# Summing the next unit's first block ahead of this unit's last gelu, in a gated MLP built from seven-product block multiplications

## The chip, the cores and the metric

The kernel runs on one core of a Trainium2 chip. The metric is the time of one execution on the device in microseconds (us). Before the change the median was 542.64 us in three runs (541.96 to 542.75).

The engines: TensorE (PE; its weight loads stand separately as PEld), VectorE (DVE), ScalarE (ACT), GpSimd (POOL), and SyncE (SP), which issues the transfers. TensorE writes its products into PSUM, which the program uses as eight banks of 128 x 512 f32; the operands of its matmuls lie in SBUF. A "slot" is one of 52 buffers of a shared pool in SBUF, used again and again. fp32r is a 4-byte float type for matmuls.

## The reference

```python
# B, S, Dm, Df = 1, 2048, 1024, 3584; all bf16
def reference(x, w_gate, w_up, w_down):
    g = jnp.einsum("bsd,df->bsf", x, w_gate)
    u = jnp.einsum("bsd,df->bsf", x, w_up)
    h = _gelu(g) * u                      # tanh form
    return jnp.einsum("bsf,fd->bsd", h, w_down)
```

## The kernel before

The rows of x are taken in two passes (`ip` 0 and 1) of 1024. Each pass first makes h, in 14 units of 256 columns of the gate and up weights, and then multiplies by the down weights. A unit is a 2 x 2 block multiplication done with seven products instead of eight: sums and differences of blocks of x (`t1` to `t4`, and the cast `tb`) are multiplied with sums and differences of weight blocks (`s1` to `s4`, and the cast `sa`). GpSimd makes the weight sums of the next unit while this one runs. Two of the seven products take raw bf16 blocks, the others take fp32r. Everything exists for gate and for up, so a "product" below is two groups of four matmuls. `p1`, `u2` and `p5` are copies of products that ScalarE takes out of PSUM (`snap`).

The down projection is done in the same way, and for it 14 slices of the down weights have to be subtracted from each other once. Most of that is hidden in the first pass: in 12 of its units, ScalarE copies three raw halves of a slice into PSUM banks that are idle just then (`keep`), and VectorE subtracts from there into `m`. The second pass does none of this.

```python
def add(ps, other):
    g = new(dve, ps[0], other[0], ADD, "sum", dtype=f32)   # gate: VectorE, into a slot
    dve(ps[1], ps[1], other[1], ADD)                        # up: VectorE, in place in PSUM
    return g, ps[1]

# ... inside unit(...): e, c, d are pairs of PSUM banks
    e, c, d = banks
    aside(-2)
    g, up = add(c, p1)                    # the unit's first block: c holds raw products
    aside(-1)
    for i in GU:
        product(e[i], s["s2"][i], t["t2"], False)
    aside(0)
    keep(0, c[0])                         # ScalarE copies raw weights into c[0], VectorE subtracts
    # ... (first unit: another order)
    g = gelu(g)                           # ScalarE
    c11 = g, up
    times(2 * u, 0, *c11)                 # VectorE multiplies into h
    u2 = [snap(e[i], "u2") for i in GU]   # ScalarE copies PSUM to SBUF
    keep(1, c[0])
    keep(2, c[1])
    c = d
    for i in GU:
        product(c[i], s["s1"][i], t["t1"], True)
    p5 = [snap(c[i], "p5") for i in GU]   # ScalarE
    after_p5()
    for i in GU:
        product(e[i], s["s3"][i], t["t3"], False)
    # ... add e and p5 (VectorE)
    for i in GU:
        product(c[i], s["s4"][i], t["tb"], False)   # the "tb products": same banks as p5's source
    times(2 * u + 1, 1, gelu(g), up)
    aside(1)
    g, up = add(c, u2)
    ahead_of_p4()                         # raw products of the NEXT unit, and its p1 copies
    for i in GU:
        product(e[i], s["sa"][i], t["t4"], False)
    times(2 * u, 1, gelu(g), up)
    aside(2)
    times(2 * u + 1, 0, gelu(e[0]), e[1]) # the unit's last gelu and multiply

def keep_part(j, part, ps):
    ra, rb = wraw[j]
    # ... (part 0 takes a new tile made[j])
    a = (ra[:, N:], rb[:, N:], rb[:, :N])[part]
    b = (ra[:, :N], made[j][:, 0], made[j][:, 1])[part]
    nc.scalar.copy(out=ps, in_=a)
    dve(made[j][:, part], ps, b, SUB)
```

VectorE and TensorE keep the order in which the program is written. ScalarE's order is set by a scheduler, in most units; it comes out as gelu, raw copy, gelu, two u2 copies, two raw copies, two p5 copies, two `sa` casts.

## Time and profile before

| | before |
|---|---|
| time, median | 542.64 us |
| PE busy, share of the span | 535.1 us, 99% |
| DVE / ACT / POOL busy | 62% / 47% / 44% |
| first-pass unit, mean of 11 | 12.62 us |
| second-pass unit, mean of 12 | 12.56 us |

From the page of the kernel before: busy time, share of the span and instructions of each engine (its part 1), and the chain of work that ended last (its part 4).

```profile
PE 535.1 (99%) x2414; PEld 379.5 (70%) x2414; DVE 334.9 (62%) x524; ACT 255.4 (47%) x463; POOL 239.2 (44%) x215
...
PE 99%; ACT 0%; DVE 0%; issue 0%
PE bank L111 98%; PE bank L502 1%; PE bank L449 0%; ACT st L413 0%; DVE warm L433 0%
```

The chain is all matmuls. But busy time cannot tell whether matmuls follow each other as fast as they could. The Trainium skill, "Perfetto Trace Analysis", section "Identifying the Most-Contended Engine", says that matmul busy share is not a good measure of how close a kernel is to its roofline, since pipelined matmuls look smaller in the trace. PE busy is 12.56 us of a 12.56 us window in a unit of either pass, although a first-pass unit takes longer. So the single records of the trace were taken, and the distance from one matmul's start to the next was worked out. It is 216 ns for bf16 and 227 ns for fp32r nearly everywhere, but not in the last product of a unit (`t4` with `sa`), which ripples between 224 and 236 ns in both passes and is taken up at the end. The tb products differ between the passes: 10 of the 12 units with down weights are like the first row. (This is not a view of the profile: the numbers are differences of start times, and times between a copy's end and a start.)

```
kernel before                    end of the two p5 copies,    the first tb load   distances of the eight starts
                                 before the first tb matmul   leads its matmul by from one to the next (ns), sum
first pass, typical unit         209 ns and -277 ns           96 ns               251 237 233 236 224 231 236 233   1881
second pass, typical unit        1766 ns and 1026 ns          224 ns              226 227 227 226 227 227 226 230   1816
```

From the waits view of the kernel before. The columns are who waited for what: us in total, times, longest.

```profile
DVE hT L90 <- PE bank L111: 43.7, 25, 1.8
...
ACT bank L274 <- DVE sum L90: 20.5, 12, 1.7
...
PEld bank L111 <- issue: 2.0, 12, 0.2
```

The last line is the leak as this view shows it: twelve times, the weight load of an fp32r product began late, and the view has no engine to name for it ("issue"). The middle line is where the lateness starts: a ScalarE copy of raw weights into a bank waits 12 times 1.7 us for VectorE's sum.

From the timeline of the kernel before, one first-pass unit. The columns are start, duration, engine, line, operation, tiles out<-in, shapes, count, and in brackets the idle time just before with what ended it.

```profile
124.57 0.60 ACT L179 ACTIVATE g<-bank 128x512 f32<-128x512 f32 x1 [1.49 <-PE bank L111]
...
125.56 0.69 DVE L90 TENSOR_TENSOR hT<-g,bank 128x512 bf16<-128x512 f32 x1 [1.75 <-PE bank L111]
126.17 0.68 DVE L90 TENSOR_TENSOR sum<-bank,p 128x512 f32<-128x512 f32 x1
126.77 0.69 DVE L90 TENSOR_TENSOR bank<-bank,p 128x512 f32<-128x512 f32 x1
126.89 0.59 ACT L274 CAST bank<-raw 128x512 f32<-128x512 bf16 x1 [1.71 <-DVE sum L90]
...
127.94 1.06 ACT L107 COPY u<-bank 128x512 f32<-128x512 f32 x2
...
128.89 1.12 ACT L274 CAST bank<-raw 128x512 f32<-128x512 bf16 x2
...
129.93 1.08 ACT L107 COPY p<-bank 128x512 f32<-128x512 f32 x2
130.64 1.70 PEld L111 LDWEIGHTS bank<-tb,s 128*128 128x128 f32 x8 [0.17 <-issue]
130.73 2.04 PE L111 MATMUL bank<-tb,s 128*128 128x512 f32 x8
```

Read it from the bottom. The tb products overwrite a bank pair that the p5 copies must have read; the second copy, which frees the second bank, starts at 130.4 us and the first at 129.93, just before the load at 130.64. The p5 copies stand behind two raw copies, those behind the u2 copies, and all of it behind the first raw copy at 126.89, which stood idle for 1.71 us until VectorE had done the sum at 126.17. The sum in turn is queued behind the multiply `hT` at 125.56, for which VectorE had itself been idle for 1.75 us.

### The profile page before, as it was taken

What the parts mean: (1) busy time and instruction counts of PE and PEld (TensorE: products, weight loads), DVE (VectorE), ACT (ScalarE), POOL (GpSimd) and SP (SyncE); (2) the same over time, 40 slices, a digit from 0 to 9 for tenths busy, and PEclk for the clock granted to TensorE, in tenths of its full rate; (3) what the DMA queues carried; (4) which work ended last, traced back from release to release, by engine and by line L of the source; (5) the groups of instructions that cost most, each with busy time, mean ns of one, the idle gap of its engine ahead of it and who ended that gap; (6) DMA issues with size and microseconds to landing.
All of it is one profiled execution on the core that took longest, in us unless ns stands there. A gap on an engine that the chain in (4) does not pass through costs nothing.

```text
span 539.8 us, 7428 instructions
## 1 busy us (share of the span) xinstructions
PE 535.1 (99%) x2414; PEld 379.5 (70%) x2414; DVE 334.9 (62%) x524; ACT 255.4 (47%) x463; POOL 239.2 (44%) x215
## 2 busy tenths in 40 slices
PE   9999999999999999999999999999999999999997
PEld 5577777666677646888877667777777775488885
DVE  2986666666666895694945545445554459676730
ACT  3556666666656410255354555454555541114431
POOL 1079966677773500000097777777766600000000
PEclk9999999999999999999999999999999999999999
DMA  9766666666664899979772232233330059573751
GB/s 247 157 181 177 175 176 191 201 185 186 200 188 141 294 379 316 301 181 292 240 195 79 78 80 78 79 88 99 101 101 4 1 167 372 182 240 92 236 183 49
DMA packets 108133, 93.28 MB, mean 173 GB/s; under 512 B 17216, under 2 KB 92992, under 8 KB 108096
## 3 DMA queue, kind: packets, MB, share of 16 engines
q1 hardware_dynamic: 108096, 92.82, 58.8%
q8 instruction: 19, 0.31, 0.2%
q14 instruction: 18, 0.15, 0.1%
HBM read 74.45 MB, written 15.20 MB: 166 GB/s over the span
## 4 chain that ended last, share of the span: by engine, by line
PE 99%; ACT 0%; DVE 0%; issue 0%
PE bank L111 98%; PE bank L502 1%; PE bank L449 0%; ACT st L413 0%; DVE warm L433 0%
## 5 line engine op out<-in xcount | busy, mean ns | idle before, releaser
L93 POOL TENSOR_TENSOR s<-w 128x512 fp32r<-128x512 bf16 x102 | 120.0, 1198 | 165.1 <-DVE t L90 86.7
L111 PE MATMUL bank<-t,s 128*128 128x512 f32 x648 | 151.7, 390 | 0.0
L111 PEld LDWEIGHTS bank<-t,s 128*128 128x128 f32 x648 | 121.6, 188 | 25.5
L90 DVE TENSOR_TENSOR hT<-g,bank 128x512 bf16<-128x512 f32 x112 | 76.7, 687 | 92.9 <-ACT g L179 46.0
L111 PE MATMUL bank<-xT,w 128*128 128x512 bf16 (+1 forms) x504 | 111.9, 376 | 0.0
L107 ACT COPY p<-bank 128x512 f32<-128x512 f32 x124 | 70.6, 593 | 77.4 <-PE bank L111 77.1
L111 PEld LDWEIGHTS <-w 128*128 128x128 bf16 x504 | 47.0, 98 | 58.5 <-issue 6.9
L179 ACT ACTIVATE g<-sum 128x512 f32<-128x512 f32 x81 | 51.4, 635 | 29.8 <-DVE sum L90 28.6
L111 PE MATMUL bank<-q 128*128 128x512 f32 x240 | 58.9, 389 | 0.0
L111 PE MATMUL bank<-t,sa 128*128 128x512 f32 x216 | 58.8, 414 | 0.0
L93 POOL TENSOR_TENSOR s<-w,s 128x512 fp32r<-128x512 bf16 x50 | 57.8, 1181 | 0.0
L93 POOL TENSOR_TENSOR s<-s,w 128x512 fp32r<-128x512 f32 x50 | 57.0, 1162 | 0.0
L90 DVE TENSOR_TENSOR sum<-bank,p 128x512 f32<-128x512 f32 x54 | 37.0, 685 | 30.5 <-PE bank L111 30.5
L111 PE MATMUL bank<-tb,s 128*128 128x512 f32 x216 | 54.0, 392 | 0.0
L111 PEld LDWEIGHTS bank<-q 128*128 128x128 f32 x240 | 45.0, 188 | 9.4
L111 PE MATMUL bank<-raw,hT 128*128 128x512 bf16 x224 | 48.7, 379 | 0.0
L111 PEld LDWEIGHTS bank<-t,sa 128*128 128x128 f32 x216 | 40.7, 188 | 10.7
L111 PEld LDWEIGHTS bank<-tb,s 128*128 128x128 f32 x216 | 39.6, 188 | 9.9 <-issue 2.0
L102 ACT CAST tb<-raw 128x512 fp32r<-128x512 bf16 x28 | 17.2, 626 | 60.0 <-DMA raw<-in_w_down_dram 26.5
L90 DVE TENSOR_TENSOR q<-hT 128x512 fp32r<-128x512 bf16 x56 | 38.4, 686 | 4.5 <-PE bank L111 4.5
L111 PEld LDWEIGHTS <-hT 128*128 128x128 bf16 x224 | 21.8, 98 | 26.5 <-issue 0.5
L90 DVE TENSOR_TENSOR bank<-bank,p 128x512 f32<-128x512 f32 x54 | 37.4, 693 | 3.1 <-PE bank L111 3.1
(45 smaller groups left out, 454.7 us busy)
## 6 DMA issues: line engine op xcount, KB each, us to landing
raw<-in_w_down_dram SPq DMA_DIRECT2D x80, 256.0 KB, 4.8
q<-td SPq DMA_DIRECT2D x60, 256.0 KB, 5.0
w<-in_w_gate_dram SPq DMA_DIRECT2D x27, 512.0 KB, 5.9
w<-in_w_up_dram SPq DMA_DIRECT2D x27, 512.0 KB, 7.0
td<-m SPq DMA_DIRECT2D x12, 768.0 KB, 4.5
w<-td SPq DMA_DIRECT2D x6, 1024.0 KB, 9.7
out_dram<-st SPq DMA_DIRECT2D x32, 128.0 KB, 1.7
td<-w SPq DMA_DIRECT2D x2, 768.0 KB, 6.6
```

What stands on the lines that cost most here:

```text
L90: nc.vector.tensor_tensor(out=out, in0=a, in1=b, op=op)
L93: nc.gpsimd.tensor_tensor(out=out, in0=a, in1=b, op=op)
L102: nc.scalar.copy(out=t, in_=src)
L107: nc.scalar.copy(out=t, in_=ps)
L111: nc.tensor.matmul(ps, lhsT=lhs, rhs=rhs, start=start, stop=stop, skip_group_check=True)
L179: nc.scalar.activation(g, src, ACT.Gelu_apprx_tanh)
L502: nc.tensor.matmul(bank[3][:, :cols], lhsT=warm[:, :P], rhs=warm[:, :cols], start=True, stop=True)
```

## The change

The intent: the sum of the next unit's first block needs only the raw products and their p1 copies, and these are complete before the last product of this unit. It is put ahead of the last gelu and its multiply, into VectorE's idle time; then ScalarE's raw copy, whose bank the sum frees, moves up as well.

```diff
-    def unit(u, banks, xT, w, s, t, p1, after_p5, aside, keep, ahead_of_p4, snap_first):
+    def add(ps, other):                       # moved out of unit, otherwise the same
+        ...
+    def unit(u, banks, xT, w, s, t, c11, after_p5, aside, keep, ahead_of_p4, behind_p4, snap_first):
         ...
-        g, up = add(c, p1)
+        g, up = c11()
         ...
         times(2 * u, 1, gelu(g), up)
-        aside(2)
+        behind_p4()
         times(2 * u + 1, 0, gelu(e[0]), e[1])
 ...
+            def behind_p4():
+                if "p1" in nxt:
+                    nxt["c11"] = add(cc, nxt["p1"])
+
+            def c11():
+                return nxt.pop("c11", None) or add(cc, p1)
```

(`aside(2)` did nothing.) No operation is added or removed; the matmuls keep their order.

More of the change, by code (lines that the diff above doesn't have):

```diff
@@ L196, in raw_products @@
         return p1
-    def unit(u, banks, xT, w, s, t, p1, after_p5, aside, keep, ahead_of_p4, snap_first):
+    def add(ps, other):
+        g = new(dve, ps[0], other[0], ADD, "sum", dtype=f32)
+        dve(ps[1], ps[1], other[1], ADD)
+        return g, ps[1]
+    def unit(u, banks, xT, w, s, t, c11, after_p5, aside, keep, ahead_of_p4, behind_p4, snap_first):
         GU = range(2)
-        def add(ps, other):
-            g = new(dve, ps[0], other[0], ADD, "sum", dtype=f32)
-            dve(ps[1], ps[1], other[1], ADD)
-            return g, ps[1]
         e, c, d = banks
         aside(-2)
-        g, up = add(c, p1)
+        g, up = c11()
         aside(-1)
@@ L576 @@
             with tc.manual_schedule(engines={ENG.Activation}) if first else nullcontext():
-                unit(u, (e, cc, dd), xT, w, s, t, p1, prepare, aside, keep, ahead_of_p4, first)
+                unit(
+                    u, (e, cc, dd), xT, w, s, t, c11, prepare, aside, keep,
+                    ahead_of_p4, behind_p4, first,
+                )
             if u + 1 < NU:
```

## The prediction

> **What bounds the kernel.** TensorE. The page gives PE busy 535.1 us of a span of 539.8 (99%), full granted clock in every slice, and a chain of waits that is 98% matmuls of one helper line. The Trainium skill, "Perfetto Trace Analysis", section "Identifying the Most-Contended Engine", says that matmul busy share is a poor measure, since matmuls are pipelined; so I read the distance from one matmul's start to the next in the timeline: 216 ns for bf16, 227 for fp32r products, nearly everywhere, with one of about 418 at each change from bf16 to fp32r. The waits view has no matmul waiting for a semaphore. VectorE (62%) and ScalarE (47%) are spare.
>
> **The one leak.** The tb products (operands tb and s) differ between the passes. In the second, their eight distances add up to 1816 ns per unit. In the first, in 10 of 12 units, to about 1880: the first is 251 ns instead of 227, the next ones 231 to 238. Two more units have about 1838. The waits view shows the weight loads before them idle for "issue", 2.0 us in 12 times: they start only 96 ns ahead of the matmul, against 224 in the second pass. (The skill's "TensorE: Matmul & The Clock Gate", "Step-by-step: what each phase is for", says weight loads are pulled ahead of matmuls in flight; this trace agrees.) Reason: these products write banks that ScalarE's p5 copies must first have read. In the second pass those copies end 1766 and 1026 ns before the first tb matmul; in the first, 209 ns before and 277 ns after it. There ScalarE also makes three copies of raw down weights per unit (598 ns each), the first of which waits 1.71 us for VectorE's sum, queued behind the multiply after the unit's last gelu. Loss, worked out: 10 x 64 + 2 x 22 = 0.7 us, 0.13%.
>
> **What the change does.** No operation is added or removed. Sum (685 ns) and add in place (690 ns) move ahead of the last multiply (687 ns), into a stretch where VectorE idles 1.75 us; their operands are complete 2 us before the old place. The sum should end before the last gelu starts. The first raw copy then follows that gelu at once, the gelu of the sum runs 1.7 us earlier, the second copy can start sooner, and the p5 copies should end about 1.1 and 0.6 us before the first tb matmul, restoring the weight load's lead.
>
> Slot reuse shifts: some sums now wait for a Pool sum as well, some Pool sums for a DMA. I traced the targets: all about a unit back, long done. Matmul order is unchanged.
>
> **On the critical path:** only the 0.7 us, all in the first pass.
>
> **Predicted time:** 542.0 us, 8-in-10 range 541.2 to 542.8. Faster by over 2%: 0.005; within 2%: 0.985; slower by over 2%: 0.01.
>
> **Signs.** Right: ScalarE's wait for the sum before the raw copy (20.5 us, 12 times) almost gone; first-pass tb products at 1817 ns; the 2.0 us of "issue" idle gone; first-pass unit period from 12.63 to 12.56 us. Wrong: tb distances stay at 251 although the p5 copies end earlier (then contention is the cause), or new distances over 240 ns elsewhere.
>
> **What would make it wrong.** The 0.7 us is near the run-to-run spread (541.96 to 542.75), so times may hide it. A misjudged slot wait could stall Pool sums, which have about 2 us of room ahead of the tb products, and so TensorE.

## The result, and the profile after

Ratios are the mean time of one kernel's fast runs over the mean of the other's in the same rounds, so they are not quite the ratio of the medians quoted.

In the first comparison the changed kernel took 541.13 us (median of 4, 540.65 to 541.99) against 542.67 us before (4 runs), ratio 0.9976, 95% interval 0.9959 to 0.9994: within 2%, and a little faster. The profiles, from single executions:

| | before | after |
|---|---|---|
| first-pass unit, mean of 11 | 12.62 us | 12.56 us |
| second-pass unit, mean of 12 | 12.56 us | 12.56 us |
| tb products, typical first-pass unit: first distance | 251 ns | 227 ns |
| p5 copies end before the first tb matmul | 209 and -277 ns | 1313 and 826 ns |
| span of the profiled run | 539.8 us | 539.9 us |

From the page of the kernel after, its part 1:

```profile
PE 533.1 (99%) x2380; PEld 381.4 (71%) x2414; DVE 334.6 (62%) x524; ACT 260.0 (48%) x463; POOL 239.2 (44%) x215
```

PE busy is not down by 2 us because anything became cheaper: this trace holds 2380 of the 2414 matmuls, and all 2414 weight loads. 34 matmul records are missing, most of them the first matmul of the raw products of the next unit. A second trace of the same kernel (the first experiment) has all 2414, and PE busy 535.3 us.

From the waits view of the kernel after:

```profile
DVE hT L90 <- PE bank L111: 13.6, 24, 0.6
...
ACT g L179 <- DVE sum L90: 7.4, 6, 1.7
PEld L111 <- issue: 7.3, 28, 0.3
```

The line of ScalarE's raw copy waiting for the sum (20.5 us) is gone, and so is the "issue" idle of the fp32r loads (2.0 us). The last line above is another group, the loads of raw bf16 weights; it stood at 7.4 us before. VectorE's multiply waits 13.6 us instead of 43.7 for TensorE, since the sum now fills that time.

From the timeline of the kernel after, one first-pass unit:

```profile
136.75 0.68 DVE L90 TENSOR_TENSOR sum<-bank,p 128x512 f32<-128x512 f32 x1
...
137.65 0.60 ACT L179 ACTIVATE g<-bank 128x512 f32<-128x512 f32 x1 [1.54 <-PE bank L111]
...
138.14 0.59 ACT L272 CAST bank<-raw 128x512 f32<-128x512 bf16 x1
...
138.57 0.69 DVE L90 TENSOR_TENSOR hT<-g,bank 128x512 bf16<-128x512 f32 x1 [0.54 <-PE bank L111]
...
140.80 1.11 ACT L272 CAST bank<-raw 128x512 f32<-128x512 bf16 x2
...
141.84 1.08 ACT L107 COPY p<-bank 128x512 f32<-128x512 f32 x2
...
143.52 1.55 PEld L111 LDWEIGHTS bank<-tb,s 128*128 128x128 f32 x7
143.74 1.52 PE L111 MATMUL bank<-tb,s 128*128 128x512 f32 x6
```

The raw copy follows the last gelu at once, the p5 copies are done by 142.9, and the first load begins 0.22 us before its matmul, with no idle time before it.

Why then are the two profiled spans the same? The stages, from the starts of matmuls in the two traces:

```
stage, us                                              before    after    difference
start of the span to the first product with x           7.00      7.89     +0.89
first product with x to the first tb product            22.85     22.82    -0.03
first to 13th tb product (units of the first pass)      151.43    150.72   -0.71
13th to 14th (last unit, down projection, new pass)     100.31    100.24   -0.07
14th to 27th tb product (units of the second pass)      163.28    163.28    0.00
27th tb product to the end of the span                  94.92     94.92     0.00
```

One line of the timeline of each kernel shows the first stage, before and then after:

```profile
7.00 3.31 PE L111 MATMUL bank<-xT,w 128*128 128x256 bf16 x22
```

```profile
7.88 2.41 PE L111 MATMUL bank<-xT,w 128*128 128x256 bf16 x17
```

The start-up, which the change does not touch, took 0.89 us longer in the one execution that was profiled. Over the seven traces here without an added copy it lies between 6.96 and 7.96 us whatever the kernel. Behind it the changed kernel gains 0.81 us, 0.78 of it between the first tb product of the first pass and that of the second.

### The profile page after: what moved, and what is told of

Same layout as the page of the kernel before. It is cut to its first block, busy times and chain, and to the rows that moved or that the text cites. A ratio compares the mean times of both kernels' runs of the same rounds, so it can differ in the third digit from the quotient of the medians.

```text
span 539.9 us, 7400 instructions
## 1 busy us (share of the span) xinstructions
PE 533.1 (99%) x2380; PEld 381.4 (71%) x2414; DVE 334.6 (62%) x524; ACT 260.0 (48%) x463; POOL 239.2 (44%) x215
## 4 chain that ended last, share of the span: by engine, by line
PE 99%; issue 0%; ACT 0%; DVE 0%
PE bank L111 97%; PE bank L500 1%; PE bank L447 1%; ACT st L411 0%; DVE warm L431 0%
## 5 line engine op out<-in xcount | busy, mean ns | idle before, releaser
L90 DVE TENSOR_TENSOR hT<-g,bank 128x512 bf16<-128x512 f32 x112 | 75.5, 685 | 67.7 <-ACT g L179 51.1
L111 PE MATMUL bank<-xT,w 128*128 128x512 bf16 (+1 forms) x476 | 106.2, 375 | 1.9
L107 ACT COPY u<-bank 128x512 f32<-128x512 f32 x62 | 35.9, 590 | 24.2 <-PE bank L111 21.8
L179 ACT ACTIVATE g<-bank 128x512 f32<-128x512 f32 x31 | 18.6, 601 | 46.0 <-PE bank L111 45.7
```

What stands on the lines that cost most here:

```text
L90: nc.vector.tensor_tensor(out=out, in0=a, in1=b, op=op)
L107: nc.scalar.copy(out=t, in_=ps)
L111: nc.tensor.matmul(ps, lhsT=lhs, rhs=rhs, start=start, stop=stop, skip_group_check=True)
L179: nc.scalar.activation(g, src, ACT.Gelu_apprx_tanh)
```

## The experiments

All outputs are right. The theory: the p5 copies ended too late for the weight load of the first tb product to be started ahead, and the change lets them end earlier. Rivals: the moved sum itself, or less interference of VectorE's subtractions and of the stores with the tb products, made the gain; or slots and transfers did, which the moved allocation also shifts.

### The changed kernel again

No edit.

> The changed kernel, unaltered, timed again in more rounds. The first comparison gave a ratio of 0.9976 (0.9959 to 0.9994), about 1.3 us less, while the trace shows only 0.8 us less between the first tb products of pass one and of pass two. Theory (the weight loads' lead restored in the first pass is all there is): ratio 0.9985, that is 0.7 to 0.8 us less, and the interval includes 0.9987. Rival (something else was gained as well, such as slots or transfers): ratio at or under 0.9976 again, with some other stage of the trace shorter than before.

Measured: 541.47 us (5 runs) against 542.52 (9 runs), ratio 0.9984, interval 0.9972 to 0.9997. The trace repeats the stages: first-pass unit 12.56 us, 531.99 us from the first product with x to the end against 532.79 before (531.98 in the first trace of the change). So the theory's 0.9985 is met, and no other stage is shorter by more than 0.03 us.

### The p5 copies first, the sum where it was

```diff
 # the kernel before
-        keep(1, c[0])
-        keep(2, c[1])
-        c = d
+        kc, c = c, d
         ...
         p5 = [snap(c[i], "p5") for i in GU]
+        keep(1, kc[0])
+        keep(2, kc[1])
         after_p5()
```

> The kernel before, with the sums where they were, but with ScalarE's two p5 copies put ahead of its second and third raw copy. Theory (late p5 copies cost the lead of the first tb weight load): p5 copies end about 1.2 and 0.7 us before the first tb product, the eight tb distances of a unit of the first pass add up to 1816 or 1817 ns instead of 1880, unit period 12.56 us, ratio to before 0.9985. Rival (the moved sum itself helps, or VectorE's m subtractions and the store of m disturb the tb products): here the m subtractions fall even more into the tb products, so distances of 231 to 238 ns stay, about 40 ns a unit or more, and the ratio is about 1.000.

Measured: 541.22 us against 542.52, ratio 0.9980 (0.9968 to 0.9993). The p5 copies end 1.25 and 0.76 us before the first tb product, all eight distances are 227 or 226 ns (230 to the next product), the unit period is 12.56 us. The raw copy still waits for the sum, as the waits view of this run shows:

```profile
ACT bank L274 <- DVE sum L90: 20.5, 12, 1.7
```

and VectorE's subtractions `m` fall right into the tb products, as the timeline of this run shows:

```profile
128.68 1.09 ACT L107 COPY p<-bank 128x512 f32<-128x512 f32 x2
129.63 1.14 ACT L274 CAST bank<-raw 128x512 f32<-128x512 bf16 x2
130.29 1.49 DVE L90 TENSOR_TENSOR m<-bank,m 128x512 fp32r<-128x512 f32 x2 [1.70 <-ACT bank L274]
130.30 1.77 PEld L111 LDWEIGHTS bank<-tb,s 128*128 128x128 f32 x8
130.53 1.98 PE L111 MATMUL bank<-tb,s 128*128 128x512 f32 x8
```

So the wait of 20.5 us was not itself the cost, and the subtractions beside the matmuls cost nothing. What matters is when the p5 copies end. This version has a new small loss: in the last unit of the first pass the weight load of the last product waited 0.35 us for VectorE's sum, late behind the subtractions; from the first product with x to the end it takes 532.28 us, 0.3 more than the change.

### The change in one pass only

```diff
-                if "p1" in nxt:
+                if "p1" in nxt and ip == 0:      # second kernel: ip == 1
                     nxt["c11"] = add(cc, nxt["p1"])
```

> The change made only in the first pass. Theory: all of the gain lies here; first-pass tb products at 1816 ns, ratio to before as that of the whole change, about 0.9985. Rival (the second pass gains too): ratio nearer to 1 than the whole change, with the second pass's unit period 12.56 us in both.

> The change made only in the second pass. Theory: no gain; first-pass tb products stay at about 1880 ns in 10 units, second-pass unit period 12.56 us as before, ratio 1.000 within 0.001. Rival: a ratio of 0.9985 or less.

Measured, first pass only: 541.29 us, ratio 0.9981 (0.9968 to 0.9995), first-pass unit 12.56 us. Second pass only: 542.51 us, ratio 1.0004 (0.9990 to 1.0017), first-pass unit 12.63 us, tb products at 1880 or 1881 ns in ten units. The second-pass unit takes 12.56 us in both, as before. All of the gain lies in the first pass. The trace of the second kernel also shows 1.0 us more in the first down projection, where two matmuls waited 0.7 us for a transfer of raw down weights; its ratio is about 1, so this is told as a thing of that execution and was not followed up.

### Late p5 copies on purpose, first try

The scheduler is turned off for ScalarE in the first pass (the order stays the same but for one pair of copies in one unit), and 1, 2 or 3 idle copies are added ahead of the p5 copies; and 1 in the kernel before.

```diff
                     keep_part(js[0], part, ps)
+                    for _ in range(1 if part == 2 else 0):     # or 2, or 3
+                        nc.scalar.copy(out=warm, in_=ps)
 ...
-            with tc.manual_schedule(engines={ENG.Activation}) if first else nullcontext():
+            with tc.manual_schedule(engines={ENG.Activation}) if ip == 0 else nullcontext():
```

> The change, plus one idle ScalarE copy per down-weight unit ahead of the p5 copies (about 0.49 us each, the step of neighbouring copies in the trace). Theory: the p5 copies then end about 0.82 and 0.34 us before the first tb product instead of 1.31 and 0.83, still early enough for a load that leads by 224 ns, so no loss: distances of 227 ns, first-pass unit period 12.56 us, ratio to before 0.998 to 0.999. Rival (any work added to ScalarE costs, or the gain came from less ScalarE work near the tb products): period over 12.58 us.

> The change, plus two such copies. Theory: the first p5 copy ends about 0.33 us before the first tb product; in the kernel before, a load started 113 ns after the first p5 copy's end, so a full lead needs 0.337 us: this is at the edge, unit period between 12.56 and 12.63 us, first load 150 to 224 ns ahead, ratio to before 0.998 to 1.000.

> The change, plus three such copies. Theory: the first p5 copy would end about 0.16 us after the undelayed start of the first tb product, so TensorE waits openly: the first product starts 209 ns after the copy's end, some 0.37 us late, and a unit loses 0.37 us plus 0.024 to 0.064 us; over 11 to 12 units 4.3 to 5.2 us more than the changed kernel, ratio to before 1.006 to 1.009. Rival (contention, not the p5 copies' end): a loss of at most 0.06 us a unit, ratio under 1.001. Side question: if the distances behind the first one are 227 here, the 231 to 238 ns seen before are not made by the late load alone.

> The kernel before, plus one such copy. Theory: there is no room left there, so one copy costs its full step: 0.49 us in each of 11 to 12 units, 5.4 to 5.9 us, ratio to before 1.010 to 1.011, while the same copy in the changed kernel costs nothing. Rival: the cost is the same in both kernels, or under 1 us.

Measured: the change with 1, 2 and 3 copies 548.02, 555.72 and 562.35 us, ratios to before 1.0104, 1.0248 and 1.0371; the kernel before with 1 copy 561.44 us, 1.0354. All four numbers miss what was expected. The waits view of the first of them says why:

```profile
ACT warm L559 <- DVE m L90: 12.4, 12, 1.0
```

The idle copy reads a bank that VectorE is subtracting from, and the program serializes the two readers. It waited 1.0 us per unit, so one copy delayed the p5 copies by about 1.6 us instead of 0.5. The error lay in the experiment, and the numbers still serve. The first-pass unit periods are 13.09, 13.71 and 14.32 us, and 14.20 for the kernel before with one copy. The same copy costs 13.09 - 12.56 = 0.53 us a unit in the changed kernel and 14.20 - 12.62 = 1.58 us in the one before; the difference of 1.05 us is, to 0.05, the 1.10 us by which the change had let the p5 copies end earlier (1313 - 209 ns).

### Late p5 copies on purpose, without the wait

The idle copy now reads raw weights in SBUF:

```diff
-                        nc.scalar.copy(out=warm, in_=ps)
+                        nc.scalar.copy(out=warm, in_=wraw[js[0]][1][:, :N])
```

> In the last four runs the idle copy read a bank that VectorE was still subtracting from, and so also waited 1.0 us per unit for VectorE: it delayed the p5 copies by about 1.5 us instead of 0.5. Here it reads raw weights in SBUF instead. The change plus one such copy per down-weight unit. Theory: the p5 copies end about 0.77 and 0.29 us before the first tb product, full lead, tb products at 1817 ns, first-pass unit period 12.56 us, ratio to before 0.998 to 0.999. Rival (any work added to ScalarE here costs): period 12.6 us or more.

> The change plus two such copies. Copies into one tile followed each other at 0.62 us in the last runs, so the first p5 copy should end about 0.15 us before the undelayed start of the first tb product. Theory: much the lateness of the kernel before (0.21 us), a little worse; a product starts at the earliest 144 ns after that copy's end, as in the last runs, and then loses up to 79 ns at the second and some 40 ns behind. Unit period 12.60 to 12.70 us, ratio to before 0.9995 to 1.0015: all of the gain lost again, with the sum still at its new place.

> The kernel before plus one such copy. Theory: no room there, the first p5 copy ends some 0.33 us after the undelayed start, so a unit takes about 0.33 + 0.14 + 0.08 + 0.04 = 0.59 us more than 12.56; period 13.08 to 13.2 us, ratio to before 1.010 to 1.013. The same copy costs nothing in the changed kernel. Rival: equal cost in both.

Measured: the change with one copy 541.64 us, ratio 0.9988 (0.9973 to 1.0003), unit 12.56 us. With two copies 543.88 us, ratio 1.0028 (1.0013 to 1.0043), unit 12.73 us. The kernel before with one copy 548.36 us, ratio 1.0113 (1.0098 to 1.0128), unit 13.13 us. The first and the third are as expected; the second loses more than expected (12.60 to 12.70), because its two copies delayed the first p5 copy so far that it ended 92 ns, not 150, before the undelayed start.

From the timeline of the change with one copy, and then with two:

```profile
128.66 0.62 ACT L559 COPY warm<-raw 128x512 bf16<-128x512 bf16 x1
129.18 1.07 ACT L107 COPY p<-bank 128x512 f32<-128x512 f32 x2
...
130.34 1.77 PEld L111 LDWEIGHTS bank<-tb,s 128*128 128x128 f32 x8
130.56 1.97 PE L111 MATMUL bank<-tb,s 128*128 128x512 f32 x8
```

```profile
130.26 1.49 DVE L90 TENSOR_TENSOR m<-bank,m 128x512 fp32r<-128x512 f32 x2 [1.03 <-ACT bank L272]
130.67 1.27 ACT L559 COPY warm<-raw 128x512 bf16<-128x512 bf16 x2
...
131.85 1.07 ACT L107 COPY p<-bank 128x512 f32<-128x512 f32 x2
...
132.54 0.53 PEld L111 LDWEIGHTS bank<-tb,s 128*128 128x128 f32 x3 [0.28 <-issue]
132.57 0.70 PE L111 MATMUL bank<-tb,s 128*128 128x512 f32 x2
```

With one copy ScalarE does more work than before the change in this stretch, and nothing is lost. With two, the "issue" idle is back, and the subtractions end at 131.75, well before the tb products. In the kernel before with one copy TensorE even waits openly, and its waits view names ScalarE at last:

```profile
PE bank L111 <- ACT p L107: 3.2, 11, 0.3
...
PEld bank L111 <- issue: 7.5, 11, 0.7
```

The runs fall on one rule, here for a typical first-pass unit (records of the traces, ns; the last column in us):

```
                                  first p5 copy ends   first tb load   first       tb start   unit
                                  before first tb mm   leads mm by     distance    is late    period
change + p5 first (told below)    1829 to 1832         223             227         0          12.56
change                            1313                 223             227         0          12.56
before + p5 first                 1248                 223             227         0          12.56
change + 1 copy                    796                 224             226         0          12.56
before                             209                  96             251         0          12.62
change + 2 copies                  144                  31             306         52         12.73
change + 1 copy that waits         144                  31             306         422        13.09
before + 1 copy                    144                  31             306         453        13.13
```

Whenever the load is late, it starts 113 or 114 ns after the first p5 copy's end (209 - 96, and 144 - 31), and it then leads its matmul by at least 30 ns. "Late" is the distance to the matmul before, less 227 ns. The sum of all this is the period: in the second row from below, for example, 422 + (306 - 227) + some 30 in the distances that follow = 0.53 us.

Two things in these traces sharpen the rule. With one idle copy and with two, VectorE's last subtraction ends 0.83 us and the store of `m` is issued 0.80 us before the first tb matmul, in both; only the kernel with two loses, so neither is the cause. And one unit, in the kernel with the change in the second pass only (at 43.13 us), shows where the edge lies: its p5 copies end 223 ns before and 266 ns after the first tb matmul, the load leads by 110 ns, and all eight distances are 226 or 227 ns (230 to the next product). At 213 ns, in the kernel before (at 42.41 us), the load leads by 99 ns and the first distance is 240 ns. So the second copy, which still reads PSUM beside the first tb matmuls in that unit, costs nothing either; but it is a single unit.

### Both at once

The change with the p5 copies ahead of the second and third raw copy (the edit of the second experiment on the changed kernel).

> The change and the p5 copies moved ahead of raw copies as well. Theory: the changed kernel has no loss left at this place, so the two do not add up: tb products 1817 ns, period 12.56 us, ratio to before 0.998 to 0.999, no better than the change alone. Rival: they add up, ratio under 0.997.

Measured: 541.14 us, ratio to before 0.9976 (0.9960 to 0.9993). That is just under the range expected, but the trace shows no further gain: unit 12.56 us, and 531.98 us from the first product with x to the end, as for the change alone. The two do not add up. This version does not beat the changed kernel beyond noise.

## Why the prediction was right

- **What bounds the kernel**: right. Matmul starts 216 and 227 ns apart remain the floor in every kernel here, and only what pushed them apart moved the time.
- **The leak, and its cause**: right, and shown, though "the one leak" says too much (see the last point). Making the p5 copies early by another edit gives the same gain with the 20.5 us wait still in place; making them late again in the changed kernel takes the gain away; adding the same copy to both kernels costs 0.51 us a unit (13.13 against 12.62) in the kernel before and nothing in the changed one. The rival that the prediction named, contention, falls: subtractions in the middle of the tb products left them at 227 ns, and the long distances came back with the subtractions out of the way; the stores fall as well (0.80 us ahead of the tb products with and without loss).
- **The size of the leak**: predicted 0.7 us from the tb products. The stages show 0.78 us between the first tb products of the two passes; the tb distances themselves give 10 x 64 + 43 = 0.68 us. The other 0.09 us, which the prediction did not have, lies in the next fp32r product, `t4` with `sa`: it took 9 or 10 ns longer in the ten units whose tb products took about 1880 ns.
- **How much earlier the p5 copies would end**: predicted 1.1 and 0.6 us before the first tb product, measured 1.31 and 0.83. It did not matter, since already 0.74 to 0.80 us is enough (the change with one copy).
- **Second pass and down projection gain nothing**: right (12.56 us in both; the change in the second pass only has ratio 1.0004).
- **Slot waits**: no new wait of TensorE for GpSimd or a transfer shows in the changed kernel's trace.
- **The time**: predicted 542.0 us, 541.2 to 542.8. The first median, 541.13, lies 0.07 us under the range; the ratio of that comparison times 542.67 is 541.37, and the repeat gave 541.47, both inside it. The gain measured was 1.54 and 1.05 us by medians, the one traced is 0.81. Every interval of the change includes 0.9985, so nothing beyond the traced gain is shown. What stays open: the runs of the kernel before fall into two clusters (for instance 541.27 and 541.33, against 542.09 to 542.92 in the other seven of that set), and the one profiled with it at first, 541.56 us, belongs near the lower. No trace of the upper cluster was taken, so what those executions spend is not known; the start-up, which varies by 1 us between traces, is a candidate that was only argued.
- Also open: why the distances behind the first stay off 227 ns (224 to 238) in most units with a late load, and return to 227 at once in a few (the unit at 80.25 us of the kernel before).
- Overlooked, and still there: in 25 of the 27 units of either kernel `t4` with `sa` follows raw bf16 products, its first load leads by only 26 or 27 ns, and the distances (from the repeat of the changed kernel) are 28, 418, 224, 231, 236, 228, 233, 230 ns: much the series behind a late tb load, though it writes other banks than those that the p5 copies read. Against one distance of 216 and seven of 227 this is some 23 ns a unit, about 0.6 us in 25 units (an estimate from these distances), nearly as much as the leak that was closed. No run tried to remove it.

## What to carry to other kernels

When TensorE is busy 99% of the span, compare the distance between matmul starts in two stages that do the same work: here a first distance that was 24 ns too long, with a late weight load before it, marked the 73 ns a unit that were the whole of this change (12,633 against 12,560 ns). Then ask which copy has to free the bank of that product, and how long before it ends; a wait of 20 us upstream costs only as far as it eats that slack, and once the slack is enough (here 0.21 us was too little, 0.22 us enough in the one unit that had it, and 0.74 us in all), more of it buys nothing. A gain of 0.15% is smaller than what the start-up does from run to run, so it is read from the stage, not from the span.

## What the Trainium skill lacked or had wrong

- "TensorE: Matmul & The Clock Gate", "Back-to-back issue gap", gives about 131 ns per matmul at N=512 as a sustained figure for pairs of weight load and matmul. Here such pairs run 216 ns apart in bf16, for hundreds of matmuls. The page's 216 ns, which it calls the isolated gap, is the one that fits.
- The same page, "Step-by-step: what each phase is for", says that weight loads are pulled ahead, and the trace agrees (223 to 224 ns of lead). It lacks that a pending bank holds the load of an fp32r product too: the load started 113 ns after the copy that freed the bank, leading by 96 or 31 ns only. In the built program an fp32r matmul has no load instruction of its own, while a bf16 one has (774 loads for 774 bf16 matmuls, none for the 1640 of fp32r).
- It gives no figures for fp32r, neither in its issue gap nor under "LDWEIGHTS (loading the stationary operand)": here starts 227 ns apart at N=512 and loads of 188 ns, against 216 ns and 98 ns for bf16.
- "Perfetto Trace Analysis" does not say that matmul records can be missing: here 34 of 2414, which lowered PE busy by 2 us and made distances of 456 ns where nothing was lost.
